# Strassen's scheme for part of a feed-forward layer's second product, with sums of the weights streamed from DRAM

## The chip, the cores and the metric

One of the eight NeuronCores of one Trainium2 chip runs the whole program. The metric is the device time of one execution in microseconds; the reference point is the median of three runs.

## What is computed

Packed attention for eight batches, then a feed-forward layer over its 4608 output rows. Cut to what matters:

```python
def _attn_ref(q, k, v, p):               # (8 batches, 8 heads, 576, 64); p: 32 rows a head
    def sm_attn(qq, kk, vv):
        s = scale * np.matmul(qq, kk.transpose(0, 1, 3, 2))
        a = np.exp(s - np.max(s, axis=-1, keepdims=True))
        a = a / (np.sum(a, axis=-1, keepdims=True) + 1e-09)
        return np.matmul(a, vv)
    p_packed = sm_attn(p, k, v)
    return sm_attn(q, p_packed, p_packed)

def _moe_ref(x, w_in, w_out):            # x (4608, 512), w_in (512, 2048), w_out (2048, 512)
    h = x @ w_in
    g = np.where(h > 0.0, h, np.exp(np.minimum(h, 0.0)) - 1.0)
    return g @ w_out
```

The two weight matrices arrive as 64-bit floating point words, which the kernel itself turns into 32-bit numbers.

## The kernel before

**Number format.** A product of the feed-forward layer is made of three matmuls on the rounded 32-bit type (`F32R`): each operand is split into a high part and a low remainder, and high by high, high by low and low by high are summed in PSUM. For the first 4 of 16 blocks of `d_ff`, in the first batches, plain 32-bit matmuls stand in their place.

**First product.** `x @ w_in` isn't formed from `x`. `mstep` makes, for each batch and each quarter of `d_ff`, a small matrix `m` (`m_hi`, `m_lo`: packed values times `w_in`), and `h` is `m` times the attention weights `a` (`a_hi`, `a_lo`): six matmuls for one block of 128 columns of `d_ff` (index `f`, 0 to 15) and one window of tokens.

**Windows.** A batch has 576 tokens in two windows: 256 and 320 in even batches, 320 and 256 in odd ones. Of 576 tokens 64 are over after four tiles of 128. The second window of an even batch therefore computes `g` for 64 more tokens and keeps them in `half_sb`; the first window of the following odd batch (`ODD_HALF`) puts them before its own 320 and so has three tiles of 128 tokens where every other window has two. A visit is a window with a range of `f`. Batches 0 and 1 are done in 13 interleaved visits, while the weights are still being converted; from batch 2 on every visit runs over all 16 `f`.

**One step of a visit.** For each `f`: `mm` (L811, matmuls on L822) makes `h` in a PSUM bank; ScalarE makes `relu(-h)` (L829) and its exponential (L835); VectorE combines them into `g` (L838), rounds it to `g_hi` (L252, the helper `copy`, on whichever of the two engines the planner chose) and takes the remainder `g_lo` (L861). `out_mm` (L928, matmuls on L938, L939 and L941) then does, for each tile of 128 tokens, three matmuls with the tile of `g` as weights and 512 columns of `w_out` as moving operand, into one PSUM bank for each tile. After the last `f` the banks are copied to `part` and stored.

**Order.** No loop order is left to a compiler. Every piece of work is an `op` with a priority in units of steps (`i`, the index of the visit's step), an estimated cost on an engine, the ops it depends on and the buffers it takes (`Ring`, and `Banks` for PSUM). `schedule` simulates engines, buffers and one DMA queue with these costs, and writes every engine's instructions in the order that comes out. `LOOK` is by how many steps `out_mm` is put behind `mm`; `T_ATT` says in which steps of the batch before the attention of a batch is done, `TM` the same of `mstep`; `LM`, `T_WS`, `T_AS` and `STAY` are further offsets of this kind. All plain DMAs are issued by SP in one order: loads of keys, values and queries into a ring of two pairs of buffers (`kvq`, L431, L438 and L442, L450), weights (L275) and stores (L966). Partial sums of batches 0 and 1 are added into `out` by DMAs that POOL issues (L964).

Of the kernel before, what the change touches and what calls it, by code (L numbers as in the profile page):

```python
# [20 lines left out]
def packed_attention_elu_ffn(  # L21
# [9 lines left out]
):  # L31

# [8 lines left out]
    nc = tc.nc  # L41
# [44 lines left out]
    T_WS, T_AS = 20, 6  # L86
# [68 lines left out]
    def schedule():  # L155
# [57 lines left out]
    parts = ctx.enter_context(tc.tile_pool(name="parts", bufs=2))  # L213
# [22 lines left out]
        kvq=2, m_hi=NFC, m_lo=NFC, m_hi_late=1, m_lo_late=1, a=2, tmp=3, g=3, e=2, part=2, h=2,  # L236
        raw=3, ex=2, sg=1, mi=2, p=2, ppT=3, pp=1, k0=1, q0=1,
    ).items()}
    R["psum"] = Banks(8)
# [4 lines left out]

    def wo(f, part):
        return wo_a[:, f, part, :] if f < NFA else pools["wo_b"][:, f - NFA, part, :]

# [14 lines left out]
    def weights(f, first, prio):  # L262
# [72 lines left out]
        ld = op(-60 + f if first and f < 4 else -44 + f / 9 if f < 2 else prio - 8, {"DMA": 1.45}, load, take=[raw])  # L335
# [33 lines left out]
    def attention(b, ts):  # L369
# [86 lines left out]
        for name, fn, bufs, t in (  # L456
            ("k", load_k, k_b, ts[0] - 6), ("v", load_v, v_b, ts[0] - 5), ("q", load_q, q_b, ts[0] - 3),
        ):
            lds[name] = []
            for n, x in enumerate(bufs):  # L460
# [22 lines left out]
        def smax1(e, g):  # L483
            if g == 0:
                sv["mx"] = small.tile([P, G], F32, tag="mx", name="mx")
# [20 lines left out]
        def srec1(e):  # L506
# [6 lines left out]
        o1 = op(ts[0], {"PE": 1.0}, s1, ld_k, take=ps1 + e1s, use=[p_b] + k_b,  # L513
                after=[prev_b.tmp_last if b > 1 else None], mode=1)
        o4s, o = [], None
        for g in range(G):
            o = op(ts[0], {"DVE": 0.76}, lambda e, g=g: smax1(e, g), [o1], use=[ps1[g]], after=[o])
            o = op(ts[0], {"DVE": 0.16}, lambda e, g=g: neg(e, g), [o])
            o4s.append(op(
                ts[0], {"ACT": 0.95}, lambda e, g=g: sexp1(e, g), [o], use=[ps1[g], e1s[g]],  # L520
            ))
# [167 lines left out]
    def mstep(b, c, part, parts_, prio, deps=()):  # L689
        st = sts[b]  # L690
        if part == 0:
            late = b >= NB0 and c == 1
            st.m[c] = [Buf(
                R[x + "_late" if late else x],
                lambda x=x: (late_pools["m"] if late else mpool).tile([P, G, FC], F32R, tag=x, name=x),
# [58 lines left out]
    sts, late_pools = {}, {}  # L754

    def end_tmp0(e):
# [3 lines left out]
        pools["wo_b"] = pools["wo_pool"].tile([P, n + 56], F32R, tag="wo_b", name="wo_b")[  # L760
# [254 lines left out]
```

## Time and profile before

| | |
|---|---|
| Median of three runs | 725.22 us (725.15 to 725.24) |
| Profiled execution, its own time | 724.5 us |
| Its span | 722.3 us |
| Mean granted TensorE clock | 0.998 |
| Busy share of the span: PE, VectorE (DVE), ScalarE (ACT) | 97%, 70%, 54% |

The span runs from the first to the last instruction that the profiler saw, and 2.2 us of the execution lie outside it. A busy share is a mean over stages that differ; matmuls overlap in the records, so the duration of one matmul is longer than what it adds to the chain, which is read from the distance between starts.

### The profile page before, as it was taken

Reading aid. Unit: us, or ns where it says so; the run is one execution under the profiler, and the core shown is the slowest. Engines: PE = TensorE matmul, PEld = TensorE weight load, DVE = VectorE, ACT = ScalarE, POOL = GpSimd, SP = SyncE. Lnnn points to the kernel's source line nnn. Section 1 sums busy time; section 2 is a strip of 40 time slices with the busy share of each in tenths; the row PEclk is TensorE's granted clock in tenths of the full one; section 3 lists DMA queues with packets and bytes.
Section 4 is the critical chain, followed back from the end, with each engine's and each line's share of the span. In section 5 each row is a group of like instructions: output and inputs, shape, how many; then the busy total and the mean of one; then the engine's idle time right before and its main releaser. Section 6 shows DMA issues by size and latency. Waiting matters only on the chain.

```text
span 722.3 us, 13401 instructions
## 1 busy us (share of the span) xinstructions
PE 699.6 (97%) x5076; PEld 557.1 (77%) x5076; DVE 504.4 (70%) x1256; ACT 387.4 (54%) x900; POOL 19.4 (3%) x27
## 2 busy tenths in 40 slices
PE   2799999999999999999999999999999999999997
PEld 1454588887778877888878887888888877888886
DVE  6999998886875587545875569555686559654453
ACT  5777888885654455434454445434454345444332
POOL 0000002110111000000000000000000000000000
PEclk9999999999999999999999999999999999999999
DMA  9846546634543430003300250001400040000010
GB/s 348 296 150 204 186 147 142 132 66 108 165 59 44 123 108 1 30 1 128 117 2 29 67 165 1 2 29 66 160 21 1 30 132 30 1 30 1 0 45 30
DMA packets 29360, 61.42 MB, mean 85 GB/s; under 512 B 2544, under 2 KB 11760, under 8 KB 29040
## 3 DMA queue, kind: packets, MB, share of 16 engines
q1 hardware_dynamic: 26272, 55.06, 22.6%
q0 software_dynamic: 3024, 5.51, 5.6%
q8 instruction: 40, 0.66, 0.4%
q14 instruction: 24, 0.20, 0.1%
HBM read 45.61 MB, written 14.94 MB: 84 GB/s over the span
## 4 chain that ended last, share of the span: by engine, by line
PE 96%; DVE 1%; DMA 1%; ACT 1%; issue 0%; SPq 0%; ACTq 0%
PE psum L822 27%; PE psum L938 18%; PE psum L939 17%; PE psum L941 17%; PE psum L932 4%; PE psum L705 4%; PE psum L815 2%; PE psum L557 2%; PE psum L531 1%; PE psum L476 1%; PE psum L602 1%; DMA k<-in_kT 1%; DVE mx L486 0%; ACT tmp L500 0%; SPq L275 0%
## 5 line engine op out<-in xcount | busy, mean ns | idle before, releaser
L829 ACT ACTIVATE e<-psum 128x256 f32<-128x256 f32 (+1 forms) x256 | 105.4, 412 | 236.2 <-PE psum L822 214.4
L838 DVE SCALAR_TENSOR_TENSOR e<-e,psum 128x256 f32<-128x256 f32 (+1 forms) x240 | 103.6, 432 | 106.8 <-ACT e L835 106.1
L822 PE MATMUL psum<-a_hi,m_hi 128*128 128x256 f32 (+1 forms) x480 | 146.5, 305 | 0.0
L822 PE MATMUL psum<-a_lo,m_hi 128*128 128x256 f32 (+1 forms) x480 | 142.0, 296 | 0.0
L822 PE MATMUL psum<-a_hi,m_lo 128*128 128x256 f32 (+1 forms) x480 | 141.9, 296 | 0.0
L861 DVE TENSOR_TENSOR g_lo<-e,g_hi 128x256 fp32r<-128x256 f32 (+1 forms) x240 | 105.3, 439 | 22.0 <-ACT g_hi L252 7.1
L835 ACT ACTIVATE e<-e 128x256 f32<-128x256 f32 (+1 forms) x256 | 114.0, 445 | 6.1
L938 PE MATMUL psum<-wo_b,g_hi 128*128 128x512 f32 x288 | 114.8, 398 | 0.0
L939 PE MATMUL psum<-wo_b,g_hi 128*128 128x512 f32 x288 | 113.6, 394 | 0.0
L822 PEld LDWEIGHTS psum<-a_hi,m_hi 128*128 128x128 f32 x480 | 90.5, 189 | 24.2 <-issue 9.6
L938 PE MATMUL psum<-wo_a,g_hi 128*128 128x512 f32 x252 | 99.4, 394 | 0.0
L939 PE MATMUL psum<-wo_a,g_hi 128*128 128x512 f32 x252 | 99.3, 394 | 0.0
L822 PEld LDWEIGHTS psum<-a_lo,m_hi 128*128 128x128 f32 x480 | 90.7, 189 | 8.7 <-issue 1.0
L822 PEld LDWEIGHTS psum<-a_hi,m_lo 128*128 128x128 f32 x480 | 90.6, 189 | 0.0
L941 PE MATMUL psum<-wo_b,g_lo 128*128 128x512 f32 x288 | 86.6, 391 | 0.0
L941 PE MATMUL psum<-wo_a,g_lo 128*128 128x512 f32 x252 | 76.1, 392 | 0.0
L938 PEld LDWEIGHTS psum<-wo_b,g_hi 128*128 128x128 f32 x288 | 54.2, 188 | 12.1 <-issue 3.6
L941 PEld LDWEIGHTS psum<-wo_b,g_lo 128*128 128x128 f32 x288 | 54.1, 188 | 12.1
L252 DVE CAST g_hi<-e 128x256 fp32r<-128x256 f32 (+1 forms) x180 | 54.0, 300 | 12.5 <-PE psum L939 3.7
L939 PEld LDWEIGHTS psum<-wo_b,g_hi 128*128 128x128 f32 x288 | 54.3, 189 | 7.6
L941 PEld LDWEIGHTS psum<-wo_a,g_lo 128*128 128x128 f32 x252 | 47.3, 188 | 10.5
L938 PEld LDWEIGHTS psum<-wo_a,g_hi 128*128 128x128 f32 x252 | 47.5, 188 | 9.4 <-ACT g_hi L252 2.5
(88 smaller groups left out, 761.3 us busy)
## 6 DMA issues: line engine op xcount, KB each, us to landing
out<-part SPq DMA_DIRECT2D x36, 256.0 KB, 2.2
raw<-in_w_in SPq DMA_DIRECT2D x16, 512.0 KB, 3.7
kvq<-in_v SPq DMA_DIRECT2D x16, 512.0 KB, 5.1
raw<-in_w_out SPq DMA_DIRECT2D x16, 512.0 KB, 3.5
kvq<-in_kT SPq DMA_DIRECT2D x14, 576.0 KB, 4.5
kvq<-in_qT SPq DMA_DIRECT2D x14, 576.0 KB, 4.6
out<-part POOLq DMA_DIRECT2D x21, 256.0 KB, 4.4
k<-in_kT SPq DMA_DIRECT2D x1, 1152.0 KB, 7.4
```

The source lines that it names most:

```text
L252: (nc.scalar.copy if e == "ACT" else nc.vector.tensor_copy)(out=out, in_=in_)
L557: nc.tensor.matmul(ps.t[cols_of(pair), g, :D], lhsT=e1T[g].t[:n, c, cols_of(pair)], rhs=values(c, h)[:n], start=(c == 0), stop=(c == NKC - 1),
L705: nc.tensor.matmul(ps.t[cols_of(pair), g, :w], lhsT=st.ppT.t[rows_of(g), pair, :], rhs=w_in_sb[rows_of(g), pair, c * FC + part * w:c * FC ...
L822: nc.tensor.matmul(ps_b.t[:, :n_tok], lhsT=m_b[x].t[:, g, o:o + P], rhs=st.a.t[y][:, g, cols], start=(n == 0), stop=(n == 3 * G - 1),)
L829: nc.scalar.activation(out=e_b.t[:, :n_tok], in_=ps_b.t[:, :n_tok], func=AF.Relu, scale=-1.0)
L835: nc.scalar.activation(out=x, in_=x, func=AF.Exp, scale=-1.0)
L838: nc.vector.scalar_tensor_tensor(out=out, in0=e_b.t[:, cs], scalar=-1.0, in1=ps_b.t[:, cs], op0=ALU.add, op1=ALU.max)
L861: nc.vector.tensor_tensor(out=g_b.t[1][:, cs], in0=x, in1=g_b.t[0][:, cs].bitcast(F32), op=ALU.subtract)
L932: nc.tensor.matmul(a.t, lhsT=g_b.t[0][:, t].bitcast(F32), rhs=w_words[f // 2].t[:, f % 2, :], start=first, stop=final,)
L938: nc.tensor.matmul(a.t, lhsT=g_b.t[0][:, t], rhs=wo(f, 0), start=first, stop=False)
L939: nc.tensor.matmul(a.t, lhsT=g_b.t[0][:, t], rhs=wo(f, 1), start=False, stop=False)
L941: nc.tensor.matmul(a.t, lhsT=g_b.t[1][:, t], rhs=wo(f, 0), start=False, stop=final)
```

## The change

In seven visits, (2, second window), (3, second), (4, both), (5, second) and (6, both), the second product is done for two blocks of `f` and two tiles of 128 tokens at a time by Strassen's scheme in Winograd's form: seven products of 128 by 128 blocks of `g` with 128 by 256 blocks of `w_out`, where the plain way has eight. The sums of blocks of `g` are made by VectorE in each pair of steps, the products are summed over `f` in four PSUM banks (before: two), and additions at the end of a visit combine the banks. Four of the seven right-hand blocks are sums of blocks of `w_out`: these are made once, written to a DRAM tensor (`sw_dram`, four tiles of 256 KB for each of eight pairs of `f`) and loaded again in every one of these visits into a ring of six tiles. Seven matmul groups are of 256 columns. Beside that: the first scores of batches 3 to 7 are done in two halves with two PSUM banks instead of one go with four; the extra buffers for `m` of `late_pools` are gone; the start's load order is a list, `FIRST`; the planner's offsets have other values; and the build is given `dynamic_dma_scratch_size=4096`.

```diff
-    T_ATT, T_ATT1 = [12, 14.0, 15.0, 16.0, 17.5, 17.5], [-12, -11, -11, -10, -10, -9]
-    LI, LO, LM, LOOK = 4.5, 3.0, 2.5, 3.5
-    TM = [24.5, 24.5, 28.0, 28.0]
-    T_S2, STAY, SWITCH = 0, 4, 0.12
+    T_ATT, T_ATT1 = [12, 14.0, 14.5, 16.5, 18.0, 18.0], [-12, -11, -11, -10, -10, -9]
+    LI, LO, LM, LOOK = 4.5, 3.0, 1.5, 3.5
+    TM = [24.5, 24.5, 28.0, 28.5]
+    FIRST = "i0 i3 o0 i2 i1 k v o1 q".split()
+    T_S2, STAY, SWITCH = 0, 1, 0.12
-    T_WS, T_AS = 20, 6
+    T_WS, T_AS = 23, 8
+    T_ATTS = [[10, 8, 13, 12, 12.5, 15.5], [-4, -2, 1, 8, 18, 24.0]]
+    TMS = [[21, 21, 23, 23], [25, 29, 31.5, 31.5]]
+    S_FIRST, T_SW, T_SL, T_SE, LOOK_S = (2, 1), 20, 3, 4, 4.5
...
+        if b < S_FIRST[0] + 1:
+            o1 = op(t, {"PE": 1.0}, s1, ld_k, take=ps1 + e1s, use=[p_b] + k_b, after=[free], mode=1)
...
+            for half in range(2):
+                ps = ps1[half]
+                o1 = op(
+                    t, {"PE": 0.52}, lambda e, half=half, ps=ps: s1_half(e, half, ps), ld_k,
...
+    def strassen_weights(u):
...
+        def words(e):
+            nc.vector.tensor_tensor(
+                out=w_b.t.rearrange("p (f e) -> p f e", f=2), in0=wo2(f, 0), in1=wo2(f, 1), op=ALU.add
...
+        prio = s_first + f - T_SW
+        x = op(prio, {"DVE": 1.15}, words, [w_ready[False, f], w_ready[False, f + 1], weights_end,
+               w_split.get(f), w_split.get(f + 1)], take=[w_b, t_b])
+        x = op(prio, {"DVE": 0.62}, t13, [x], use=[w_b, t_b])
+        x = op(prio, {"DVE": 0.7}, t24, [x], use=[w_b, t_b])
+        for n, b in enumerate(sw):
...
+            y = op(prio, {"ACT": 0.37}, high, [x], take=[b], use=[t_b], after=[run.get("sw")])
+            run["sw"] = y
+            y = op(prio, {"DVE": 0.36}, low, [y], use=[t_b, b])
+            s_ready[u, n] = op(prio, {"DMA": 0.7}, store, [y], use=[b])
...
+    def strassen(b, win):
+        return S_FIRST <= (b, win) < (B - 1, 1) and (b % 2, win) != ODD_HALF
...
+    def strassen_pair(i, b, win, f):
...
+        if not half:
+            ps_b, h_b = banks(1), Buf(R["h"], lambda: None)
+            x = op(
+                i, {"PE": 0.714 * 2}, lambda e: [h_mm(ps_b.t[:, n * 2 * P:(n + 1) * 2 * P], n) for n in range(2)],
...
+        def sums(e):
+            for out, x, y, o in ((4, 0, 2, ALU.add), (6, 1, 0, ALU.subtract),
+                                 (5, 4, 1, ALU.subtract), (7, 3, 5, ALU.subtract)):
+                nc.vector.tensor_tensor(out=blocks(out), in0=blocks(x), in1=blocks(y), op=o)
...
+        x = op(i + 1, {"DVE": 0.84}, sums, done, use=[w8])
+        x = run["g"] = op(i + 1, {"ACT": 0.95}, hi, [x], take=[g_b], use=[w8], after=[run["g"]])
+        x = op(i + 1, {"DVE": 1.09}, lo, [x], use=[g_b, w8])
...
+            ld[n] = run["sw"] = op(
+                i - T_SL, {"DMA": 0.7}, load, [s_ready[u, n]], take=[sw[n]], after=[run["sw"]]
+            )
...
+        groups = (
+            ((1, own(f, 0)),),
+            ((5, t(2)), (3, own(f + 1, 0))),
+            ((6, t(1)), (4, t(0))),
+            ((2, t(3)), (7, own(f + 1, 1))),
+        )
...
+                    for k, (p, q) in enumerate(((0, 0), (0, 1), (1, 0))):
+                        x0 = (7 * p + blk - 1) * P
+                        nc.tensor.matmul(
+                            a.t[:, n * H:(n + 1) * H], lhsT=g_b.all[:, x0:x0 + P], rhs=y(q),
...
+            run["out"] = op(
+                i + 1 + LOOK_S, {"PE": 0.355 * len(group)}, mm, [x] + [ld[n] for n in ns],
...
+            y = op(q, {"ACT": 0.35, "DVE": 0.4}, first, [acc[0].last], take=[part], use=acc[:1])
+            y = op(q, {"DVE": 0.69}, add1, [y, acc[1].last], use=[part, acc[1]])
+            y = op(q, {"DVE": 0.69}, add2, [y, acc[2].last], use=[part, acc[2]])
+            y = op(q, {"DVE": 0.42}, add3, [y], use=[part, acc[2]])
+            y = op(q, {"DVE": 0.69}, add4, [y, acc[3].last], use=[part, acc[3]])
...
-    nc = bacc.Bacc("TRN2", target_bir_lowering=False, num_devices=1)
+    nc = bacc.Bacc("TRN2", target_bir_lowering=False, num_devices=1,
+                   dynamic_dma_scratch_size=4096)
```

In the second window of an even batch (320 tokens) `strassen_pair` makes `h` and `g` step by step as before and writes the 64 tokens over to `half_sb`; the two tiles of 128 go into the pair's eight blocks. `hi` rounds seven blocks (896 columns) at once and `lo` takes their remainders.

## Rows read from the trace of the kernel before

**Rows 1.** The page: engines' busy time, and their tenths in 40 slices.

```profile
span 722.3 us, 13401 instructions
PE 699.6 (97%) x5076; PEld 557.1 (77%) x5076; DVE 504.4 (70%) x1256; ACT 387.4 (54%) x900; POOL 19.4 (3%) x27
...
PE   2799999999999999999999999999999999999997
...
DVE  6999998886875587545875569555686559654453
```

**Rows 2.** The page: the chain that ended last.

```profile
PE 96%; DVE 1%; DMA 1%; ACT 1%; issue 0%; SPq 0%; ACTq 0%
```

**Rows 3.** Timeline of PE in the last visit: start, duration, line.

```profile
690.60 0.28 PE L822 MATMUL psum<-a_hi,m_hi 128*128 128x256 f32 x1
690.72 0.28 PE L822 MATMUL psum<-a_lo,m_hi 128*128 128x256 f32 x1
...
691.32 0.40 PE L938 MATMUL psum<-wo_a,g_hi 128*128 128x512 f32 x1
691.55 0.39 PE L939 MATMUL psum<-wo_a,g_hi 128*128 128x512 f32 x1
...
692.70 0.29 PE L822 MATMUL psum<-a_hi,m_hi 128*128 128x256 f32 x1
```

**Rows 4.** Chain of waits, in order of time: first scores of a batch, between steps.

```profile
325.34 1.13 PE psum L476 x32
326.47 1.08 PE psum L822 x6
...
329.61 0.88 PE psum L822 x6
```

**Rows 5.** Groups of instructions by line and shape: busy us, mean ns, idle before.

```profile
L861 DVE TENSOR_TENSOR g_lo<-e,g_hi 128x256 fp32r<-128x256 f32 x180 | 76.0, 422 | 19.1 <-ACT g_hi L252 5.8 <-PE psum L941 2.0 <-DVE g_hi L252 0.8
L838 DVE SCALAR_TENSOR_TENSOR e<-e,psum 128x256 f32<-128x256 f32 x180 | 74.6, 414 | 68.3 <-ACT e L835 67.6
...
L835 ACT ACTIVATE e<-e 128x256 f32<-128x256 f32 x128 | 53.5, 418 | 3.0
...
L252 DVE CAST g_hi<-e 128x256 fp32r<-128x256 f32 x132 | 38.6, 293 | 12.2 <-PE psum L939 3.7 <-PE psum L531 0.5
...
L252 ACT COPY part<-psum 128x512 f32<-128x512 f32 x46 | 25.9, 583 | 9.0 <-PE psum L941 8.6 <-PE psum L932 0.3
L252 ACT CAST m_hi<-psum 128x1024 fp32r<-128x1024 f32 x24 | 23.6, 1017 | 18.3 <-PE psum L705 18.3
...
L861 DVE TENSOR_TENSOR g_lo<-half_sb,g_hi 128x64 fp32r<-128x64 f32 x60 | 13.3, 222 | 24.3 <-PE psum L941 23.9
...
L252 DVE COPY part<-psum 128x512 f32<-128x512 f32 x11 | 7.6, 689 | 3.6 <-PE psum L941 3.4
```

**Rows 6.** Busy time by stage: PE, PEld, DVE, ACT, POOL, clock, DMA share, GB/s.

```profile
165.60:298.00 132.40, 132.34 (x1096) 106.29 (x1083) 94.05 (x240) 70.64 (x162) 8.68 (x10) 1.00 0.34 80
298.00:398.00 100.00, 100.00 (x711) 83.13 (x710) 63.71 (x158) 45.41 (x111) 0.00 (x0) 1.00 0.16 55
398.00:469.00 71.00, 71.00 (x549) 57.22 (x548) 48.51 (x130) 35.23 (x81) 0.00 (x0) 1.00 0.19 60
```

**Rows 7.** VectorE's groups in the stretch from 165.6 to 298 us.

```profile
L252 DVE CAST g_hi<-e 128x256 fp32r<-128x256 f32 x38 | 11.2, 294 | 3.0 <-PE psum L939 1.2
...
L331 DVE TENSOR_TENSOR wo_b<-mi,wo_b 128x512 fp32r<-128x512 f32 x1 | 0.7, 686 | 0.0
```

**Rows 8.** The page: DMA queue and issues (KB each, us to landing).

```profile
q1 hardware_dynamic: 26272, 55.06, 22.6%
...
out<-part SPq DMA_DIRECT2D x36, 256.0 KB, 2.2
...
kvq<-in_kT SPq DMA_DIRECT2D x14, 576.0 KB, 4.5
```

**Rows 9.** SP's queue: what its next DMA stood waiting for (us in total, times, longest).

```profile
SPq L966 <- ACT part L252: 288.5, 16, 45.6
SPq L438 <- PE psum L476: 164.2, 7, 48.0
```

**Rows 10.** Timeline of the start: SP's first loads.

```profile
0.74 1.34 SPq L275 DMA_DIRECT2D raw<-in_w_in  x3
2.12 0.43 SPq L427 DMA_DIRECT2D p<-in_pT  x1
2.59 0.64 SPq L429 DMA_DIRECT2D k<-in_kT  x1
6.12 0.33 SPq L275 DMA_DIRECT2D raw<-in_w_in  x1
```

More of the change, by code (lines that the diff above doesn't have):

```diff
@@ L333, in low @@
             )
-        ld = op(-60 + f if first and f < 4 else -44 + f / 9 if f < 2 else prio - 8, {"DMA": 1.45}, load, take=[raw])
+        name = ("i" if first else "o") + str(f)
+        t = FIRST.index(name) - 60 if name in FIRST else prio - 8
+        ld = op(t, {"DMA": 1.45}, load, take=[raw])
         x = op(prio, {"DVE": 0.42}, exponent, [ld], take=[ex_b], use=[raw])
@@ L511, in srec1, with s1_half @@
             nc.vector.reciprocal(out=sv["ri"], in_=sv["ri"])
[L513 to L521, printed above, removed]
+        def s1_half(e, half, ps):
+            for pair in range(NPAIR):
+                for g in range(G):
+                    nc.tensor.matmul(
+                        ps.t[cols_of(pair), g, :HS], lhsT=p_b.t[rows_of(g), pair, :],
+                        rhs=keys(pair)[rows_of(g), half * HS:(half + 1) * HS],
+                        start=True, stop=True,
+                    )
@@ new lines, in smax1_half, with keep, neg_both @@
+        def smax1_half(e, half, ps):
+            if half == 0:
+                sv["mx"] = small.tile([P, 2, G], F32, tag="mx", name="mx")
+            nc.vector.tensor_reduce(
+                out=sv["mx"][:, half, :], in_=ps.t[:, :, :HS], axis=AX.X, op=ALU.max
+            )
+        def keep(e, half, ps, g):
+            copy(e, flat(e1s[g])[:, half * HS:(half + 1) * HS], ps.t[:, g, :HS])
+        def neg_both(e):
+            for x in ("nb", "sm"):
+                sv[x] = small.tile([P, G], F32, tag=x, name=x)
+            nc.vector.tensor_tensor(
+                out=sv["nb"], in0=sv["mx"][:, 0, :], in1=sv["mx"][:, 1, :], op=ALU.max
+            )
+            nc.vector.tensor_scalar(
+                out=sv["nb"], in0=sv["nb"], scalar1=-SCALE, scalar2=None, op0=ALU.mult
+            )
@@ L691, in mstep @@
         if part == 0:
-            late = b >= NB0 and c == 1
             st.m[c] = [Buf(
-                R[x + "_late" if late else x],
-                lambda x=x: (late_pools["m"] if late else mpool).tile([P, G, FC], F32R, tag=x, name=x),
+                R[x], lambda x=x: mpool.tile([P, G, FC], F32R, tag=x, name=x),
             ) for x in (("m_hi",) if b in H_PLAIN and c == 0 else ("m_hi", "m_lo"))]
@@ L790, in packed_attention_elu_ffn @@
             else:
-                late = [weights_end] if c == 1 else []
-                mstep(b, c, 0, 1, first_use["b", b] - NS + TM[c], late)
-    half_op, half_free, stores = {}, {}, {}
-    acc, prev_out, taker = None, None, {"h": None, "e": None, "g": None}
+                t = TM if b <= S_FIRST[0] else TMS[b % 2]
+                mstep(b, c, 0, 1, first_use["b", b] - NS + t[c])
+    s_first = next(i for i, (b, half, _) in enumerate(order) if (b, half) == S_FIRST)
+    s_ready = {}
+    run = dict.fromkeys(("acc", "out", "h", "e", "g", "sw", "w8"))
@@ L877, in packed_attention_elu_ffn @@
         x1 = op(
-            i, {"PE": cost}, mm, [need, need_a], take=[ps_b, h_b], use=m_b + [a_b], after=[taker["h"]],
+            i, {"PE": cost}, mm, [need, need_a], take=[ps_b, h_b], use=m_b + [a_b], after=[run["h"]],
         )
@@ L883, in packed_attention_elu_ffn @@
             i, {"ACT": 0.44 if long else 0.385}, relu, [x1], take=[e_b], use=[ps_b, h_b],
[L884 removed]
+            after=[run["e"]],
         )
@@ L904, in packed_attention_elu_ffn @@
             last, taken = half_free[b - 1, f][-1:], []
-        into = dict(take=taken, use=[] if taken else [g_b], after=[taker["g"]] if taken else [])
+        into = dict(take=taken, use=[] if taken else [g_b], after=[run["g"]] if taken else [])
         x4 = op(
@@ L941, in out_mm @@
                 nc.tensor.matmul(a.t, lhsT=g_b.t[1][:, t], rhs=wo(f, 0), start=False, stop=final)
-        prev_out = op(
+        prev_out = run["out"] = op(
             i + LOOK, {"PE": (0.9 if g_whole else 0.693) * n_t}, out_mm,
-            last + [w_split.get(f) if not g_whole and f < F_PLAIN else w_ready[False, f], prev_out],
-            take=acc if first else [], use=[g_b] + ([] if first else acc),
+            last + [w_split.get(f) if not g_whole and f < F_PLAIN else w_ready[False, f]],
+            take=acc if first else [], use=[g_b] + ([] if first else acc), after=[run["out"]],
         )
```

246 lines of the change are left out of this document (230 added, 16 removed).

## The prediction

> **What bounds the kernel now.** I read the page first: TensorE (PE) is busy 97% of the span, VectorE 70%, ScalarE 54%, and PE's tenths stand at 9 from the third of 40 slices to the last but one [rows 1]. Busy is no proof for an engine whose records overlap, so the chain of waits comes next: 96% of it is PE [rows 2]. The table by stage says the same of each stretch after 165.6 us: 132.3 of 132.4, 100 of 100, 71 of 71 us [rows 6]. The reader is to see that nothing but matmuls sets the end between the start and the tail: a microsecond of matmuls taken out there is worth a microsecond as long as no other engine falls behind. That engine can only be VectorE: it is busy 94.1 of 132.4 us up to 298, 63.7 of 100 and 48.5 of 71 in the two batches behind, which repeat to the end [rows 6].
>
> **What a matmul adds.** Starts, not durations: six 256-column matmuls run from 690.60 to 691.32, which is 0.120 us each (records say 0.28), and six of 512 columns from there to 692.70, 0.230 each (records say 0.40) [rows 3]. Each of them has a weight load of its own: 5076 loads to 5076 matmuls [rows 1].
>
> **The gain on PE.** A pair of steps in a changed visit has now 2 steps x 2 tiles x 3 = 12 matmuls of 512 columns, 2.76 us. After: 7 products x 3 = 21 of 256 columns, 2.52 us. The first product stays. So 0.24 us a pair, not the eighth of 2.76 (0.35) that the scheme suggests: a 256-column matmul costs 0.005 us more than half a 512-column one, and there are 21 of them. Seven visits x 8 pairs = 56 pairs: **-13.4 us**. The last digit of the starts leaves the two prices open by about 0.001 us each, so -12 to -15.
>
> Here one rule of the Trainium skill speaks against the change. TensorE: Matmul & The Clock Gate, section Back-to-back issue gap, gives for a sustained stream of weight load and matmul pairs about 81 ns at 128 columns and about 131 ns at 512, so far less than in proportion. By an estimate on the straight line between the two, 98 ns at 256, a pair would go from 12 x 131 = 1.57 to 21 x 98 = 2.06 us, and the 56 pairs would cost 27 us. The trace doesn't agree at 512 columns, where it has 230 ns. Without the page: the shape that the change multiplies runs in this kernel already, with its load, at 0.120 us [rows 3], and what would be new is only that weights are blocks of `g` and no longer of `m`.
>
> **More turns on PE.** First scores of batches 3 to 7 come in two goes with two banks. After one go the next six matmuls take 1.08 us, otherwise 0.88 [rows 4], so a turn costs about 0.2 us: 5 x 0.2 = **+1.0** (0 to 2, as `STAY` 1 for 4 lets PE turn more often elsewhere).
>
> **VectorE in a changed pair.** Before, for two steps: `g` 2 x 0.414, remainder 2 x 0.422, and rounding 0.293 each where VectorE does it [rows 5]: 1.67 to 2.26 us. The groups of 64 and 256 columns, 0.222 and 0.422 [rows 5], give 1.04 ns a column and 0.155 us fixed. After: `g` for 512 columns 0.70 (0.414 and 256 more columns at 1.1 ns), four sums of 128 columns at 0.29, less where neighbours overlap, say 0.96 (0.84 to 1.16), remainder of 896 columns 1.09: 2.75 us, and 3.3 us in the windows with 320 tokens, where `g` stays in steps and 64 tokens more are done. PE needs 12 x 0.120 + 2.52 = 3.96 us for such a pair, so alone VectorE fits in (69%). ScalarE does relu and exponential of 512 columns (about 0.6 each, from 0.418 and 0.583) and rounding of 896 (0.95, from 1.017 for 1024) [rows 5]: 2.2 of 3.96 us, hidden. From the first product to the remainder a pair takes 0.6 + 0.63 + 0.7 + 0.96 + 0.95 + 1.09 = 4.9 us plus hand-overs; `LOOK_S` puts some two pairs (8 us) of PE's work between, so this latency is covered.
>
> **VectorE in its stages.** Batch 4 (398 to 469), both windows changed: 48.5 us now; +1.1 to 1.2 for each of 16 pairs is +18.4, less 6 for some 21 roundings that go to ScalarE; the end of a visit is a chain of four additions (about 2.5) for copies of 0.689 that ScalarE did for the most part [rows 5], +4; the offsets move scores and half of `mstep` of the odd batch out, -4. That makes 61 (59 to 65) of 71 - 3.8 = 67 us: 91%. Batch 6 is the same. Up to 298 us it is tighter, since the sums of `w_out` are made there: for each of eight pairs 1024 columns (1.22), 512 (0.69), two of 256 (0.84) and four remainders of 256 (1.69), 4.4 us by the rows, 35.5 in all. They can begin when the last weight is converted; the only conversion left in this stretch is one remainder [rows 7]. 94.1 + 35.5 + 8 x 1.2 + 2.5 = 141.7 us, less up to 11 for 38 roundings that ScalarE can take (it has 70.6 of 132.4) [rows 6, 7], less 2.4 for `mstep` that may fall behind 298, less some 6 for overlap of neighbours: 122 to 131 of 131 us. VectorE is full there, and where VectorE is full PE waits now and then. I take **+3** for this stretch (0 to 9: nothing if the sums slip into holes, 9 if the sum is at its upper end and a few per cent can't be filled) and **+1** for each of batches 4 and 6 (0 to 3): +5.
>
> **DMA.** A pair needs four tiles of 256 KB, 1.05 MB in 3.96 us. The hardware queue moved 55.06 MB in 22.6% of 16 engines' 722.3 us [rows 8], 337 GB/s while busy, so 3.1 us: it fits (79%), with 20 of every 100 us for the rest. A ring of six tiles lets two of the next pair's loads start at once and two only as this pair's tiles come free, one pair (3.96 us) before their use. Stores of this size land after 2.2 us, loads of 576 KB after 4.5 [rows 8]; so there are 1.8 us to spare, and the spare is gone when two loads of keys or values (1.18 MB, 3.5 us) are queued just ahead: up to 1.8 us each at some six places (keys, values, queries of batches 5 and 7). Even batches load theirs in a window with three tiles, where no sums are needed. I take **+1** (0 to 10).
>
> **What costs nothing.** Writing the sums (8.4 MB, 32 stores) falls where the DMA share is 0.34 [rows 6]; its cover is that nobody needs a tile before its pair, and without it the first changed visit would start late. At the start SP issues three weight blocks, then the keys, because the fourth block waits for a buffer [rows 10]; the new list changes which three, not that, so the first scores begin as before. The other offsets (`T_WS`, `T_AS`, `LM`) only reorder VectorE's work there: 0 (-1.5 to +1.5). Accumulating PSUM: four banks plus two for `h` leave two for attention, which is why scores are halved; at the end of a visit the first bank is copied three groups (2 us) before the last group ends, so the next visit finds its first two banks: 0. The extra `m` buffer: `m` of an even batch now waits for the quarter before it to be used, and its offsets place it behind that: 0.
>
> **Sum.** -13.4 + 1.0 + 5 + 1 = -6.4 us against the profiled execution's 724.5, whose span leaves 2.2 us outside that the change doesn't touch; the median stands 0.7 above it. 725.2 - 6.4 = **718.8 us**, 0.9% faster. Its own bounds: -15 + 0 + 0 + 0 - 1.5 = -16.5, so 709; and with the stages' upper ends, of which I let half come together, about -13.4 + 1 + 8 + 3 = -1.4, 724.
>
> **The rivals.**
> *PE sheds its matmuls and nothing else moves.* For: VectorE never reaches its limit in the table by stage now. Against: the sums of `w_out`. -13.4 + 1.0 = 712.8, with the start's share 711 to 714.
> *VectorE becomes the bound.* The sum for 165.6 to 298 at its upper end and without relief from ScalarE, 141.7 - 2.4 of 131: +8; batches 4 and 6 at 65 of 67 with one part in fifteen unusable: +2 to 3 each. -13.4 + 1 + 8 + 5 = +0.6: 726, no change. For: rows 6 and the fixed 0.155 us of a small operation. Against: roundings can go to ScalarE, and PE has two pairs of lead.
> *SP's queue ends on the other side.* Loads of sums stand in one order with stores and key, value and query loads, and SP stands at such a DMA until its data or buffer is ready: 288 us in 16 waits for copies to `part` and 164 us in 7 for the scores [rows 9]. Today nothing urgent is behind them. After, PE is: a head of the queue that is late by more than the 1.8 us to spare stops PE. About 19 heads lie in the changed visits (7 + 6 stores, 6 loads). If each costs 1.2 us, +23 - 12.4 = +10: 735, slower; it decides from 0.65 us each. For: order is fixed ahead by estimated costs. Against: the same order puts loads as far ahead as the ring lets them.
> *Weight loads hold PE* (the rule of the Trainium skill above says it). In this kernel's terms: from 0.131 us for a 256-column matmul with weights of `g` the gain is gone (21 x 0.131 = 2.76), and at 0.140 it is 56 x (2.94 - 2.76) + 1 = +11: 736. Against it stand the rows.
>
> **How the numbers follow.** Changes within 0.2% (1.5 us) can't be told from none. Forecast 0.58; PE alone 0.17; VectorE the bound 0.13; SP's queue 0.11; weight loads 0.01. The first two are faster, the forecast's upper end not quite (0.04 to same); VectorE's case splits into faster, same and slower at 0.05, 0.04 and 0.04. So faster 0.76, same 0.08, slower 0.16. The forecast alone spans 713 to 724. The range reaches to PE alone below and through VectorE's case above, and leaves SP's: 710.5 to 727.
>
> **What would show it.** Right: in the timeline of a changed visit 21 matmuls at 0.120 us distance; PE still over 95% of the chain; holes of PE behind VectorE between 200 and 300 us. Wrong: PE waiting for `sw` loads, with SP standing at stores or `kvq` loads before them (SP's queue); VectorE over 95% busy in batches 4 and 6 too (VectorE the bound); distances over 0.125 us (weight loads). What would make the number wrong without a mechanism is the sum for VectorE up to 298 us, the one that has two ends 9 us apart.

## The result: 0.34% slower, and the profile after

The changed kernel takes 727.71 us (median of 17 runs, 724.76 to 730.49) beside 725.15 us of the kernel before (17 runs beside them). The ratio is 1.0034, 95% interval 1.0021 to 1.0047: +2.5 us, where 718.8 was forecast. It lies 0.7 us above the range, and on the other side of no change. TensorE's clock at the start, which differs from execution to execution (last section), doesn't make the difference: among executions with a mean granted clock of 0.997 or more the median is 725.2 us before (60 of 129 executions, run beside the experiments) and 727.4 after (4 of 17).

The page of the kernel after: engines, tenths of PE and VectorE, the hardware queue, the chain.

```profile
span 722.6 us, 14801 instructions
...
PE 693.3 (96%) x5580; PEld 571.4 (79%) x5580; DVE 574.3 (79%) x1377; ACT 431.3 (60%) x932; POOL 19.2 (3%) x27
...
PE   2799999999999999999999999999999999999997
...
DVE  7989998978899999845997889855797889865463
...
q1 hardware_dynamic: 63024, 122.18, 51.0%
...
PE 88%; DMA 7%; DVE 2%; ACT 1%; issue 1%; SPq 0%; ACTq 0%
```

PE is busy 6.3 us less than in [rows 1], VectorE 70 us more, and DMA, 1% of the chain in [rows 2], is 7% of it. The profiled execution took 724.76 us and is the fastest of the 17, 3.0 us below their median, so its span stands beside the old one as if nothing had been lost. The stages show what was won and lost inside this execution; what the median has more is in no trace of this kernel. The same table as [rows 6], cut where the changed kernel's visits end:

```profile
60.00:165.60 105.60, 104.08 (x612) 78.67 (x611) 95.43 (x222) 86.00 (x202) 9.78 (x11) 1.00 0.52 139
165.60:224.50 58.90, 57.22 (x522) 42.32 (x520) 51.72 (x124) 37.74 (x92) 7.00 (x8) 1.00 0.65 162
224.50:304.40 79.90, 79.31 (x667) 68.43 (x666) 72.83 (x189) 53.19 (x123) 1.73 (x2) 1.00 0.74 236
...
404.00:472.10 68.10, 67.55 (x575) 61.49 (x574) 58.85 (x144) 40.77 (x74) 0.00 (x0) 1.00 0.82 264
```

The kernel before, up to its last product of batch 0:

```profile
60.00:165.60 105.60, 105.45 (x611) 79.58 (x617) 93.05 (x219) 86.29 (x202) 9.98 (x11) 1.00 0.54 138
165.60:217.80 52.20, 52.14 (x495) 40.92 (x482) 39.96 (x98) 31.51 (x72) 6.95 (x8) 1.00 0.48 106
```

Up to 224.5 us PE now has holes (1.5 and 1.7 us idle), which it didn't have. The last product of batch 0 starts at 224.5 us, in the old trace at 217.8: 6.7 us are lost before the first changed visit, and at that place there is no block product yet. (PE's other work done by then is the same but for 16 small matmuls of first scores, 0.6 us by PE's timeline.) Behind it the changed visits win them back in this execution: the end of (4, second) is 3.1 us late (472.1 for 469.0), that of (6, second) 0.7 (640.2 for 639.5). So the loss that the trace shows is not where the forecast looked for one.

The block products themselves, from PE's timeline in visit (4, second):

```profile
439.77 0.52 PE L1090 MATMUL psum<-sw,g 128*128 128x256 f32 x3
440.13 0.51 PE L1090 MATMUL psum<-wo_a,g 128*128 128x256 f32 x3
440.48 1.24 PE L1090 MATMUL psum<-sw,g 128*128 128x256 f32 x9
441.55 0.52 PE L1090 MATMUL psum<-wo_a,g 128*128 128x256 f32 x3
```

From 439.77 to 441.55 there are 15 products: 0.119 us each. The price was right.

PE's waits for DMA after (us in total, times, longest). PEld are weight loads and PE the matmuls behind them, which wait less. In the old trace PE's weight loads don't wait for queries at all.

```profile
PEld psum L687 <- DMA kvq<-in_qT: 4.8, 5, 2.2
PEld psum L1090 <- DMA sw<-sw_dram: 4.2, 8, 1.0
...
PE psum L687 <- DMA kvq<-in_qT: 2.6, 4, 1.3
...
PE psum L1090 <- DMA sw<-sw_dram: 0.7, 2, 0.5
```

### The profile page after: what moved, and what is told of

Read it like the earlier page. It is cut to its first block, busy times and chain, and to the rows that moved or that the text cites. A ratio compares the mean times of both kernels' runs of the same rounds, so it can differ in the third digit from the quotient of the medians.

```text
span 722.6 us, 14801 instructions
## 1 busy us (share of the span) xinstructions
PE 693.3 (96%) x5580; PEld 571.4 (79%) x5580; DVE 574.3 (79%) x1377; ACT 431.3 (60%) x932; POOL 19.2 (3%) x27
## 4 chain that ended last, share of the span: by engine, by line
PE 88%; DMA 7%; DVE 2%; ACT 1%; issue 1%; SPq 0%; ACTq 0%
PE psum L1090 18%; PE psum L1179 13%; PE psum L979 12%; PE psum L1295 10%; PE psum L1296 10%; PE psum L1298 10%; PE psum L1289 4%; PE psum L788 4%; DMA kvq<-in_qT 3%; DMA sw<-sw_dram 3%; PE psum L642 2%; PE psum L1172 2%; PE psum L616 1%; PE psum L687 1%; DMA k<-in_kT 1%; PE psum L546 1%
## 5 line engine op out<-in xcount | busy, mean ns | idle before, releaser
L1090 PE MATMUL psum<-sw,g 128*128 128x256 f32 x672 | 103.2, 285 | 1.0 <-DMA sw<-sw_dram 0.7
L1090 PEld LDWEIGHTS psum<-sw,g 128*128 128x128 f32 x672 | 89.3, 188 | 9.0 <-issue 4.3
L1179 PE MATMUL psum<-a_hi,m_hi 128*128 128x320 f32 (+1 forms) x256 | 79.6, 311 | 0.4 <-DVE e L1195 0.4
L1179 PE MATMUL psum<-a_lo,m_hi 128*128 128x320 f32 (+1 forms) x256 | 76.0, 297 | 0.0
L1179 PE MATMUL psum<-a_hi,m_lo 128*128 128x320 f32 (+1 forms) x256 | 76.0, 297 | 0.0
L1295 PE MATMUL psum<-wo_b,g 128*128 128x512 f32 x176 | 70.8, 403 | 0.0
L1296 PE MATMUL psum<-wo_b,g 128*128 128x512 f32 x176 | 69.4, 395 | 0.0
L979 PE MATMUL psum<-a_hi,m_hi 128*128 128x256 f32 (+1 forms) x224 | 67.0, 299 | 0.3 <-DVE w L986 0.3
L979 PE MATMUL psum<-a_lo,m_hi 128*128 128x256 f32 (+1 forms) x224 | 65.8, 294 | 0.0
L979 PE MATMUL psum<-a_hi,m_lo 128*128 128x256 f32 (+1 forms) x224 | 65.7, 293 | 0.0
L1295 PE MATMUL psum<-wo_a,g 128*128 128x512 f32 x140 | 55.5, 396 | 0.0
L1296 PE MATMUL psum<-wo_a,g 128*128 128x512 f32 x140 | 55.2, 394 | 0.0
L1298 PE MATMUL psum<-wo_b,g 128*128 128x512 f32 x176 | 52.7, 395 | 0.0
```

The lines of the kernel that those rows point to most:

```text
L979: nc.tensor.matmul(ps, lhsT=m_b[p].t[:, g, o:o + P], rhs=st.a.t[q][:, g, cols], start=(n == 0), stop=(n == 3 * G - 1),)
L1090: nc.tensor.matmul(a.t[:, n * H:(n + 1) * H], lhsT=g_b.all[:, x0:x0 + P], rhs=y(q), start=f == 0 and n == k == 0, stop=last and k == 2 and ...
L1179: nc.tensor.matmul(ps_b.t[:, :n_tok], lhsT=m_b[x].t[:, g, o:o + P], rhs=st.a.t[y][:, g, cols], start=(n == 0), stop=(n == 3 * G - 1),)
L1295: nc.tensor.matmul(a.t, lhsT=g_b.t[0][:, t], rhs=wo(f, 0), start=first, stop=False)
L1296: nc.tensor.matmul(a.t, lhsT=g_b.t[0][:, t], rhs=wo(f, 1), start=False, stop=False)
L1298: nc.tensor.matmul(a.t, lhsT=g_b.t[1][:, t], rhs=wo(f, 0), start=False, stop=final)
```

## The experiments

Each ratio is to the kernel before, run beside it; us are (ratio - 1) x 725.2. By the intervals a difference of two rows is uncertain by 1.5 to 2.4 us. e3 and e4 leave out what the output needs.

| run | built on | edit | ratio, 95% interval | us |
|---|---|---|---|---|
| the change | | | 1.0034 [1.0021, 1.0047] | +2.5 |
| e1_no_strassen | after | second product plain everywhere | 1.0123 [1.0098, 1.0147] | +8.9 |
| e3_no_stream | after | sums not loaded | 0.9988 [0.9971, 1.0005] | -0.9 |
| e4_no_sums | after | sums neither made, stored nor loaded | 0.9972 [0.9953, 0.9991] | -2.0 |
| e7_plain_old_attention | e1 | attention of all batches as batch 2 | 1.0095 [1.0074, 1.0116] | +6.9 |
| e8_plain_all_old | e7 | all old but buffers and scratch | 1.0048 [1.0029, 1.0067] | +3.5 |
| e9_no_late_m | before | no late `m` pair | 1.0018 [1.0004, 1.0032] | +1.3 |
| e10_other_buffers | e8 | late `m` pair back, buffers of the sums gone | 1.0028 [1.0013, 1.0043] | +2.0 |
| e13_no_pad | before | `wo_b` moved by 224 bytes | 1.0026 [1.0009, 1.0044] | +1.9 |
| e18_no_pad_again | before | the same | 1.0036 [1.0021, 1.0050] | +2.6 |
| e5_issue_order | before | new order rule of `out_mm` | 1.0029 [1.0015, 1.0043] | +2.1 |
| e12_old_rule | after | old order rule | 1.0084 [1.0059, 1.0108] | +6.1 |
| e2_old_offsets | after | old offsets | 1.0087 [1.0061, 1.0113] | +6.3 |
| e6_old_rule_offsets | after | both old | 1.0025 [1.0007, 1.0043] | +1.8 |
| e11_mixed_plan | after | both old in batches 0 and 1 only | 1.0008 [0.9992, 1.0024] | +0.6 |
| e14_pad | after | `wo_b` back by 224 bytes | 1.0030 [1.0008, 1.0052] | +2.2 |
| e15_mixed_pad | e11 | `wo_b` back by 224 bytes | 0.9960 [0.9945, 0.9976] | -2.9 |
| e16_pool_loads | after | sums loaded by POOL's queue | 1.0071 [1.0042, 1.0099] | +5.1 |
| e17_mixed_pad_pool | e15 | sums loaded by POOL's queue | 1.0015 [0.9998, 1.0032] | +1.1 |

**What the block products are worth.** e1 leaves them out and keeps the rest of the change:

```diff
-    for u in range(NF // 2):
-        strassen_weights(u)
...
-        return S_FIRST <= (b, win) < (B - 1, 1) and (b % 2, win) != ODD_HALF
+        return False
```

> The changed kernel with the second product of all visits done the plain way: no sums of w_out are made, stored or loaded, no block products; the new offsets, the start's load list, the halved scores and the smaller buffers stay. Theory A (the loss sits in what is done beside the block products): the new offsets alone cost some 3 us up to 160 us and the halved scores 1 us, so 728 to 730 us. Theory B (the loss sits in the streamed tiles and SP's queue): without them and without the block products it is at the kernel before plus 1 us for the halved scores, 725 to 726.5.

+8.9 us, more than either theory has: what stands around the products, which the forecast had at +1 and some zeros, eats more than half of the 13.4 us they were to bring. e3 and e4 keep the block products and take the traffic away (they multiply blocks of `w_out` where the sums belong):

```diff
-                nc.sync.dma_start(out=sw[n].t.bitcast(F32), in_=sw_dram[u, n])
+                pass
...
-            return n, lambda part: sw[n].t[:, part * H:(part + 1) * H]
+            return n, lambda part: wo(f, part)[:, n % 2 * H:(n % 2 + 1) * H]
```

> The changed kernel with the planner's order kept and the 224 loads of the sums left out: the block products read blocks of w_out itself in place of the four sums, so the output lacks what the sums would add. The sums are still made and stored. Theory B: PE no longer waits for tiles, and kvq loads have the queue for themselves: 722 to 724 us, and the scatter over runs goes back to that of the kernel before. Theory A: 726.5 to 727.5.

e4 empties in addition `words`, `t13`, `t24`, `high`, `low` and `store`.

> As the kernel without the loads, and the sums of w_out are not made or stored either (VectorE's and ScalarE's work for them is left out, the planner's order kept); the block products read blocks of w_out. Theory C (VectorE's extra 30 us between 165 and 265 us hold PE up): 3 us below the kernel without the loads. If VectorE's extra work is hidden: the same as the kernel without the loads within 1 us.

e3 and e4 lie between their theories. The three together: block products with their sums of `g`, -10.9 (e4 less e1); making and storing sums of `w_out`, +1.2 (e3 less e4), which is not more than the uncertainty; loading them, +3.3 (the change less e3). The pages of e3 and e4 say what making takes from VectorE:

```profile
PE 695.1 (96%) x5580; PEld 573.2 (79%) x5580; DVE 574.1 (79%) x1377; ACT 431.4 (60%) x932; POOL 19.2 (3%) x27
```

```profile
PE 693.4 (96%) x5580; PEld 571.9 (79%) x5580; DVE 546.5 (76%) x1313; ACT 422.0 (59%) x900; POOL 19.2 (3%) x27
```

27.6 us, where the forecast had 35.5.

**The queue or the bandwidth?** e16 issues the 224 loads on POOL's queue, so that nothing on SP stands behind them:

```diff
-                nc.sync.dma_start(out=sw[n].t.bitcast(F32), in_=sw_dram[u, n])
+                nc.gpsimd.dma_start(out=sw[n].t.bitcast(F32), in_=sw_dram[u, n])
```

> The changed kernel, with the 224 loads of the sums issued by GpSimd's queue in place of SyncE's. Theory of the forecast's rival SP's queue (loads that wait for a free tile, 160.9 us in 164 waits, hold up the loads of q, k and v behind them, and S2 waits 7.4 us for q): S2's waits for DMA go to 0 to 2 us, and 724 to 726 us. Rival (the bandwidth is the price, or GpSimd issues a 256 KB load too slowly): 727 to 735 us, with the waits for sw longer than the 4.9 us of now.

It costs 2.7 us more than the change (and e17 below, with the same edit, 4.0 more than e15). PE's waits in e16:

```profile
PEld psum L1090 <- DMA sw<-sw_dram: 6.5, 11, 1.3
PEld psum L687 <- DMA kvq<-in_qT: 5.5, 5, 3.2
```

Queries are as late as before, though no load of sums is ahead of them. e3, which loads no sums, and e4, which doesn't store any either, wait as long:

```profile
PEld psum L687 <- DMA kvq<-in_qT: 5.5, 5, 3.3
```

```profile
PEld psum L687 <- DMA kvq<-in_qT: 5.5, 5, 3.1
```

So it is not the traffic of the sums on SP's queue that holds the queries. A load of sums lands after the same time on either queue (the rows of the change and of e16):

```profile
sw<-sw_dram SPq DMA_DIRECT2D x224, 256.0 KB, 3.9
```

```profile
sw<-sw_dram POOLq DMA_DIRECT2D x224, 256.0 KB, 3.8
```

So the queue's theory falls: off SP's queue the loads are waited for longer, not less. What the landing time goes with can be worked out from the issues and landings in the change's trace: a load of sums issued with at most one other DMA in flight lands after 2.7 us (median of 28 loads), with four others after 4.2 (57), with six others after 5.3 (12). That agrees with loads being slow because 264 GB/s move in these stages (the stage table); bandwidth alone was not tried, nor was what POOL's issuing (122 us of its time in e16, 0.55 us a load) adds to e16.

**What the rest costs.** e7 and e8 undo the rest of e1 by parts: first the attention (the new `T_ATT` and `TM` of batch 2 and scores in one go for all batches), then the rule of `out_mm` (explained below), the start list and all offsets, by the minus lines of the change's diff.

```diff
-        if b < S_FIRST[0] + 1:
+        if True:
...
-            ts = [first_use["b", b] - NS + t for t in (T_ATT if b <= S_FIRST[0] else T_ATTS[b % 2])]
+            ts = [first_use["b", b] - NS + t for t in T_ATT]
```

> The plain form of the changed kernel (733.6 us) with the attention of batches 3 to 7 at the offsets of batch 2 and the scores in one go. If the plain form lost by T_ATTS, TMS and the halved scores: 726 to 728. Theory P: 731 to 733.5.

> The plain form of the changed kernel with old offsets, old rule, old attention: what is left of the change are the buffers (m without the late pair, part, the larger g tiles) and the smaller ring of POOL's DMAs. If these cost nothing: 725 to 726.5. If the m buffer or POOL's ring is to blame: 728 to 733.

So of 8.9 us, 2.0 go with the attention (within the uncertainty, 2.4), 3.4 with rule and offsets (uncertain by 2.0), and 3.5 stay when only buffers and the DMA scratch are left of the whole change.

**The buffers, first: the late `m` pair.** The late pair is one more pair of buffers for `m` (`late_pools`), used from batch 2 on for the second quarter of `d_ff`. e9 takes it from the kernel before, e10 gives it back to e8.

```diff
-            late = b >= NB0 and c == 1
+            late = False
```

> The kernel before, of which one thing is taken away: the extra buffer of the second m step (the late pair), so that this step waits until the buffer of the first is free, as in the changed kernel. Theory (the missing buffer keeps two m steps from standing together, and each that stands alone pays a turn of TensorE of about 0.43 us; 7 to 8 batches): 728.5 to 729.5 us, and in the trace m steps one at a time. Rival (the buffer is not needed, since the planner puts the steps elsewhere at no price; the 4 us of the run with only the other buffers come from the smaller DMA scratch, the larger g tile or the part banks): 725 to 726.5 us.

> The run with the plain second product, old offsets, old rule and old attention (729.6 us), and the late pair of m buffers put back in the place of the buffers of the sums. What then differs from the kernel before is the g tile of 14 blocks, the two banks of one part tile, the two columns of mx and the DMA scratch of 4096 bytes. Theory (the late pair is the price): 725 to 726.5 us. Rival (scratch or layout are the price): 728.5 to 730 us. If both this run and the one without the late pair come out near 727, the two share it.

+1.3 and +2.0: the pair and what is left in e10 share the 3.5 us. In e8 the instructions of PE, VectorE and ScalarE stand in the order of e9, so the 2.2 us between these two don't come from the order. What the pair does is seen in the chain, in batch 4, `mstep` between products; the old trace first:

```profile
435.46 1.02 PE psum L705 x16
436.48 0.43 PE psum L938
436.91 0.24 PE psum L939
...
441.22 1.88 PE psum L705 x32
443.10 1.07 PE psum L822 x6
...
452.34 1.02 PE psum L705 x16
```

And e9:

```profile
440.10 1.02 PE psum L705 x16
...
445.85 1.02 PE psum L705 x16
446.87 0.43 PE psum L936
447.30 0.23 PE psum L937
...
456.12 1.02 PE psum L705 x16
...
466.37 1.02 PE psum L705 x16
```

With the late pair of buffers two steps run together, 1.88 us. Without it each runs alone, 1.02 us, and the product after it takes 0.43 for 0.23: 2 x 1.22 for 1.88 + 0.19 (six products after it take 1.07, otherwise 0.88), so 0.37 us for each two steps that are split. Of the eight such twos in the old chain after 200 us, e9 keeps two: 6 x 0.37 = 2.2 us, within the interval of its +1.3 (0.3 to 2.3). The chain of the changed kernel has none left: the 21 steps that it shows after 200 us all stand alone.

**The buffers, second: 224 bytes.** With the late pair back, these three engines have in e10 the order of the kernel before, and it still loses 2.0 us. In its trace only products with `wo_b` are longer, those with `wo_a` are not. The diff has one line for that tile which neither the forecast nor the description above noticed:

```diff
-        pools["wo_b"] = pools["wo_pool"].tile([P, n + 56], F32R, tag="wo_b", name="wo_b")[
+        pools["wo_b"] = pools["wo_pool"].tile([P, n], F32R, tag="wo_b", name="wo_b")[
```

e13 and e18 are the kernel before with this line alone changed; e18 is there for its trace.

> The kernel before, with one number changed: the tile wo_b is 224 bytes a partition shorter (n for n + 56), so that it lies 224 bytes further on in SBUF, as in the changed kernel. Nothing else differs, the order of all instructions included. Theory (the place of wo_b costs TensorE time: in the run with the late pair back the 512-column products with wo_b had distances of 0.233 and 0.235 us, in the kernel before 0.231 and 0.227, 288 of each, which is 0.6 + 2.3 less what the means give back): 1.5 to 2.5 us more, 727 to 728.5. Rival (the DMA scratch of 4096 bytes or the one g tile do it): 725 to 726.5 us.

> The kernel before without wo_b's 224 bytes, run again for its profile, since the profiled execution of the first was at half the TensorE clock. Theory (place of wo_b): the time 1.0 to 2.5 us above the kernel before again, and products with wo_b at 0.233 and 0.235 us beside 0.231 and 0.227, all others as before. Rival (the first time was chance): no difference, and the same distances.

Groups by line and shape (busy us, mean ns), the kernel before:

```profile
L938 PE MATMUL psum<-wo_b,g_hi 128*128 128x512 f32 x288 | 114.8, 398 | 0.0
L939 PE MATMUL psum<-wo_b,g_hi 128*128 128x512 f32 x288 | 113.6, 394 | 0.0
...
L941 PE MATMUL psum<-wo_b,g_lo 128*128 128x512 f32 x288 | 86.6, 391 | 0.0
L941 PE MATMUL psum<-wo_a,g_lo 128*128 128x512 f32 x252 | 76.1, 392 | 0.0
```

And e18:

```profile
L938 PE MATMUL psum<-wo_b,g_hi 128*128 128x512 f32 x288 | 115.6, 402 | 0.0
L939 PE MATMUL psum<-wo_b,g_hi 128*128 128x512 f32 x288 | 113.7, 395 | 0.0
...
L941 PE MATMUL psum<-wo_b,g_lo 128*128 128x512 f32 x288 | 87.9, 395 | 0.0
L941 PE MATMUL psum<-wo_a,g_lo 128*128 128x512 f32 x252 | 76.1, 392 | 0.0
```

Products with `wo_b` are 4 ns longer on two of the three lines, 2 x 288 x 4 ns = 2.3 us, and the same with `wo_a` are not. That settles which buffer; why its place matters is open. The 1.9 and 2.6 us of e13 and e18 leave, within the uncertainty, nothing of e10's 2.0 for the DMA scratch, the larger `g` tile or `part`. In the changed kernel fewer such products are left (176 on each line). Putting the bytes back (e14) shortens them by 1.4 us in all in the trace, but the time shows no difference that can be told:

> The changed kernel with the 224 bytes of wo_b put back. Theory (its plain visits have 176 x 3 products with wo_b, of which two in three are 2 to 8 ns shorter): 0.8 to 1.8 us less, so 725.5 to 727 us beside 727.7. Rival (the buffers of the sums lie elsewhere too, and the block products lose what the plain ones gain): no change, 727 to 728.5 us.

**Rule and offsets.** In the kernel before, `out_mm` is put into the order when the last `out_mm` has *ended* in the planner's simulation (`prev_out` is one of its dependencies); the change only asks that it has been *issued* (`after=[run["out"]]`). e5 moves this one item in the kernel before.

```diff
-            last + [w_split.get(f) if not g_whole and f < F_PLAIN else w_ready[False, f], prev_out],
-            take=acc if first else [], use=[g_b] + ([] if first else acc),
+            last + [w_split.get(f) if not g_whole and f < F_PLAIN else w_ready[False, f]],
+            take=acc if first else [], use=[g_b] + ([] if first else acc), after=[prev_out],
```

> The kernel before with one thing of the change alone: the planner holds a step's second product back only until the one before it is issued, and no longer until it has ended. Theory P (the planner's order of the first 16 visits, which this rule and the offsets write, costs what the plain form of the changed kernel loses): 728 to 732 us. If the loss comes from buffers, the POOL ring or the attention offsets: 725 to 726.5.

+2.1 us. In the stretch from 60 to 84 us PE then waits for `g`, which comes too late for the order that was written (waits in e5):

```profile
PEld psum L815 <- DVE g_hi L838: 2.5, 2, 1.8
...
PEld psum L932 <- DVE g_hi L838: 1.2, 1, 1.2
```

The kernel before has there:

```profile
PEld psum L815 <- DVE g_hi L838: 0.7, 1, 0.7
```

But the rule is no plain loss. Undone in the changed kernel it makes it 3.6 us slower, and the old offsets alone make it 3.8 us slower, which neither theory of e2 had; both old are about as the change itself, 0.7 us below it, so e6's theory of some 6 us failed. In e6's trace batch 0 does end at 220.0 us, 4.5 before the change's, but visit (4, second) ends at 474.0, 1.8 behind it: the early gain is lost again. (e12 puts `run.get("out")` back among the dependencies; e2 takes the minus lines of the offsets in the diff of the change, `T_ATT` and `TM` for batch 2 and the others throughout, and the old start list; e6 does both.)

> The changed kernel with one line undone: a plain visit's out products are again put into the order only after the last ones have ended, not after they have been issued. All offsets are the new ones. Theory (the rule costs by itself about the 2.0 us that it cost in the kernel before): 725 to 726.5 us. Rival (the offsets were chosen for the new rule, so that undoing it alone breaks the order): 728 to 732 us.

> The changed kernel with the old values of the start's load order, T_ATT, TM, LM, STAY, T_WS and T_AS; the block products, the sums and their own offsets stay. Theory A: the 3 us lost up to 160 us come back, 724 to 725. Theory B: within 1 us of the changed kernel, 727 to 728.5.

> The changed kernel, block products and streamed sums included, with the old rule for the plain visits (a second product waits for the end of the one before) and the old offsets up to batch 2. Theory P: the order up to 210 us is that of the kernel before, so some 6 us come back, 719 to 723 us. Else 727 to 732, as with the old offsets alone (731.7).

Rule and offsets belong together, and the effects of single edits don't add. By these traces the new ones lose in the visits of batches 0 and 1 and win in those behind. e11 takes each where it is good: in batches 0 and 1 (the first 64 steps) the old rule, start list, `STAY`, `LM`, `T_WS` and `T_AS`, the new rule, `STAY` and attention offsets behind.

```diff
+            + [run.get("out")] * (b < NB0),
...
-                        if x.mode == mode and x.prio < o.prio + STAY and engine_for(x) == "PE":
+                        if x.mode == mode and x.prio < o.prio + (4 if o.prio < 64 else STAY) and engine_for(x) == "PE":
```

> The changed kernel, with the old plan where its block products have not begun: in batches 0 and 1 a plain visit's out products wait again until the last ones have ended, STAY is 4 for the first 64 visits, and the start list, LM, T_WS and T_AS are the old ones; the later offsets and all block products stay. Theory (what is lost before the first block products comes from the planner's rule and offsets there, 2 to 6 us of the 6.7 us): 720 to 725 us, and visit (2,0) ends 3 us earlier or more. Rival (the loss there is that of buffers and of the work on the sums, which stay): 727 to 729 us.

As fast as the kernel before, and between its theories: 1.9 us below the change, hardly more than the uncertainty, with visit (2, first) ending 2.9 us earlier (261.7 for 264.6 us). Then two versions were to beat both, with the 224 bytes, and with and without POOL's queue:

> A version meant to beat both kernels: the mixed plan (726.4 us), with wo_b's 224 bytes and with the loads of the sums on GpSimd's queue. If the three add up (-1.3 by the mixed plan, -1 by the padding, -2 to -3 by the queue): 722 to 724 us. If GpSimd's queue is slower: 727 us or more.

> The mixed plan with wo_b's 224 bytes put back, its loads of the sums on SyncE's queue. If the version with GpSimd's queue lost by the queue, as the changed kernel did by 3.4 us: 724.5 to 726 us, which is below the kernel before by at most 1.5. If the padding gives nothing, as it gave the changed kernel nothing that could be measured: 726 to 727.5 us.

e17 doesn't, 727.69 us. e15 does, and by more than either theory said: 723.46 us, 0.9960 of the kernel before, some 0.7% below the change. Part of that is its start: 9 of its 12 executions have a mean granted clock of 0.997 or more, and their median, 723.5 us, is 1.7 below the 725.2 of the kernel before at such clocks and 3.9 below the change's 727.4. Visit (2, first) ends at 260.2 us in its trace, in the changed kernel's at 264.6, and its waits for DMA are these:

```profile
PEld psum L1090 <- DMA sw<-sw_dram: 4.8, 9, 0.8
...
PE psum L1090 <- DMA sw<-sw_dram: 3.0, 7, 0.6
...
PEld psum L687 <- DMA kvq<-in_qT: 0.6, 2, 0.3
```

0.6 us for queries, where the change has 4.8 (2.2 of them at 191.7 us, before the first changed visit): these waits came mostly with the new plan of the first batches, not with the sums. PE itself waits 3.0 us for sums in this trace and 0.7 in that of the change's fastest execution. e15 is 3.5 us better than e11; its `wo_b` rows are 1.6 us shorter in all. At clocks of 0.997 or more the two are 1.4 us apart (723.5 and 724.9, the latter the median of 3 executions), so the rest may well be the start's clock.

## Why the prediction was wrong, by its steps

The two kernels' difference, as a path of one-part steps: buffers +3.5, rule and offsets +3.4, attention +2.0, block products -10.9, making sums +1.2, loading them +3.3; together +2.5. Each step is uncertain by 1.5 to 2.4 us, and another order of steps would give other parts, since single edits don't add.

- **What costs nothing** is the step that failed. It had "The other offsets ... 0 (-1.5 to +1.5)" and "The extra `m` buffer: ... 0", and was silent on the planner's rule and on the 224 bytes. Measured: +3.5 for buffers and +3.4 for rule and offsets, 6.9 us on this path. From the other end, in the changed kernel itself, it is less: rule and offsets undone throughout give 0.7 us (e6), undone in batches 0 and 1 alone and with the bytes put back 5.4, or 3.9 at like clocks (e15). What it said of the start held: the first scores begin at 10.18 us, before at 10.15. For the `m` buffer it asked only whether steps would wait, not whether two would still stand together; [rows 4] had the price of a turn in view.
- **The gain on PE**, -13.4: the prices held (0.119 us for a 256-column product, forecast 0.120). In place it is -10.9, a figure that also has VectorE's work for the pairs and at a visit's end in it, for which the forecast had +2 (batches 4 and 6): -11.4 forecast, so nothing is missing here.
- **More turns on PE**, +1.0: +2.0 with the new offsets, not told apart from the forecast.
- **VectorE in its stages**, +5: its load was right (58.9 of 68.1 us busy in batch 4, forecast 61 of 67; 124.6 of 138.8 where the sums are made, forecast 122 to 131 of 131). For the stretch of the sums it had +3; making and storing them is +1.2 (uncertain by 1.8), and the holes of PE behind VectorE that were to show there are 0.4 of the 2.3 us that PE idles from 165.6 to 304.4 us, while 1.9 are waits for queries.
- **DMA**, +1 (0 to 10): +3.3. It counted with 2.2 us from issue to landing, that of stores in the old kernel [rows 8]; loads take 3.9 us while 264 GB/s move, which leaves 0.1 of the 1.8 us to spare.
- **The rivals.** PE alone falls, since DMA is 7% of the chain and the sum came out at +2.5. VectorE the bound falls too: its sign was over 95% busy in batch 4, and it is 86%. SP's queue had the sign but not the place: PE did wait for `sw` and `kvq`, 4.2 and 4.8 us on its weight loads, yet with the loads of sums off SP's queue in e16 the waits stayed. Weight loads fall by the timeline. By the figures of the Trainium skill (TensorE: Matmul & The Clock Gate, section Back-to-back issue gap) the estimate was 98 ns at 256 columns; the trace has 119 and doesn't agree. Of the signs of being right the distance of 0.120 us came, while PE is 88% of the chain and not over 95%, and the holes behind VectorE are small.

The sum was off by 8.9 us: 6.9 from the zeros, 0.5 from the pairs (-10.9 for -11.4), 1.0 and 2.3 from turns and DMA, less 1.8 for the stretch of the sums. Of these the zeros and the loads are clear of the uncertainty.

## What to carry to other kernels

When a change clears room for new buffers or replaces a planner's rule, build the old algorithm with the new surroundings first: here the surroundings cost 8.9 us, and the algorithm earned 6.4 net of making and loading its sums. A tuned order is worth several tenths of a per cent; keep it wherever the new algorithm doesn't run. Read every line of a diff for what it moves in memory, padding too.

## What was not expected of the hardware

- 224 bytes in the place of a moving operand cost 4 ns on a 512-column product on two of three lines (402 and 395 ns for 398 and 391), 0.3% of the kernel (1.9 and 2.6 us in two measurements). No run shows the cause.
- TensorE's granted clock falls to half (1.2 of 2.4 GHz) once near the start, for a time that differs from execution to execution. Windows of PE at the start, the kernel before, then e18 (us, PE busy, clock, DMA share, GB/s):

```profile
0.00:28.00 28.00, 11.85 (x219) 1.00 0.94 347
28.00:40.00 12.00, 10.00 (x112) 0.86 0.70 236
```

```profile
0.00:28.00 28.00, 11.74 (x203) 1.00 0.89 329
28.00:40.00 12.00, 9.77 (x124) 0.57 0.64 220
```

  A mean of 0.86 in 12 us is 3.4 us at half clock, one of 0.57 is 10.3; the engine was busy less than half of the 28 us before, waiting for the first loads. e18's first visit ends 3.7 us later than that of the kernel before (53.6 for 49.9), of which half of the 6.9 us more at half clock is 3.5. The 17 runs of the kernel before scatter by 4.7 us (724.03 to 728.77), and the clock goes with it: of the 129 executions beside the experiments, the 60 with a mean granted clock of 0.997 or more have a median of 725.2 us, the 29 with 0.993 or less one of 727.9. Single executions of two kernels can't be compared more closely than that without their clocks. One execution, the profiled one of e13, stood at a mean granted clock of 0.562, near half, from 100 us to its end and took 1163.95 us; its ratio leaves it out.
